# Turning a unit's maxima with VectorE's block transpose in place of a transposing matmul, and writing the rows with eight DMAs

## The chip, the cores and the metric

The kernel runs on one core of a Trainium2 chip. The metric is the device time of one execution in microseconds, the median of several runs. TensorE is called PE here, VectorE DVE, ScalarE ACT, GpSimd POOL, and SyncE, which issues nearly all DMAs, SP.

## The reference

Three things are computed from one input `x` (2048 x 640, float32): multi-head attention with 32 heads of 20 columns, a Fourier mixing (a DFT along the columns and one along the rows, real part), and a sigmoid gate that mixes the two.

```python
qkv = (x @ wqkv).reshape(B, S, 3, H, Dh).transpose(2, 0, 3, 1, 4)
scores = jnp.einsum("bhqd,bhkd->bhqk", q, k) * (Dh ** -0.5)
p = _softmax(scores, axis=-1)
a = (p @ v, heads joined) @ wo
...
y = jnp.einsum("ts,bse->bte", dft_seq_re, a_) - jnp.einsum("ts,bse->bte", dft_seq_im, b_)
return g * a + (1 - g) * y
```

What matters for the change is the softmax: the maximum of each row of scores is needed before the exponentials of that row.

## The kernel before

Attention is cut into 32 **units**, each for two heads (one in partitions 0 to 63, the other in 64 to 127) and half of the 2048 queries. Each unit's scores are computed twice.

The first time (`s_mm`, L158, the kind "m"), queries lie in the partitions: a 60-row matmul gives 128 queries by 512 keys, and DVE reduces it to one maximum per query (L170, into `mx`). A unit takes 32 steps of two such matmuls. When the last is done, `max_nm` (L184) reduces the four partial maxima of each query and negates them: `nm`, 128 partitions by 16 columns, a column for each head h and query tile q.

The second time (`score`, the kind "e", L830), keys lie in the partitions and queries in the columns, so that the exponentials come out as the attention product needs them. The maximum is subtracted inside the matmul: the stacks `qst` (queries) and `kst` (keys) have 62 rows per head there, of which rows 60 and 61 of `kst` are ones and rows 60 and 61 of `qst` hold the negated maximum, split into a rounded part and its remainder, so that no precision is lost in the float32r format. ACT then takes the exponential (L832) and PE multiplies with the values in 16 `av` matmuls (L494).

Between the two stands `max_chain` (L199), which the change touches. It must turn `nm`, which has queries in partitions, into rows of 1024 queries. It takes a PSUM bank, transposes `nm` on PE against an identity (L202), splits the 16 x 128 result in two on DVE (`split`, L108: a copy at L112 and a subtraction at L113, into `m1` and `m2`, which the profile names `m`), and lets SP write each head's eight rows of 128 into row 60 or 61 of `qst` (`rows`, L207 to L211): four DMAs per unit.

The order of the work is written out by hand. A **cycle** is one pass over `ORDER` (L36): eight half-steps of kind "e", eight of kind "m", fifteen fillers "F" (three matmuls or so of the DFT or the output product at a time) and at the end a **burst** "B" (L836). There are 256 cycles; a unit is eight of them. "m" runs 41 steps ahead of "e". In a burst come, in this order: `max_nm` for a unit whose maxima ended, up to two read-outs of finished DFT sums (`run_extras`; on DVE they are L355, L595 or L658), the 16 `av` matmuls, and then `max_chain`. So PE's transpose stands behind the `av` matmuls and ahead of the next cycle's scores. `rows` is issued two steps later, which in SP's own order means as soon as the split is done, because SP runs ahead and waits there. The rows are needed by the "e" step 32n of their unit n, late in the second cycle after the burst.

The scores use five PSUM banks in rotation (`bank`, L122); the transpose takes a place in it. A score of kind "m" gives its bank back when DVE has reduced it, one of kind "e" when ACT has taken its exponentials.

POOL does the preparation for the DFT along the rows: sums and splits of the loaded DFT tiles and of the intermediate tiles (L465, L112 and L113 with POOL, L479, L673), all in SBUF, and the normalisation of the attention output (L524). A hidden DFT fills PE in the first 54 cycles; in these POOL has little to do.

The first unit is turned before the cycles begin; there `max_chain` runs one step after the unit's end and the rows are written at once.

Of the kernel before, what the change touches and what calls it, by code (L numbers as in the profile page):

```python
# [10 lines left out]
F32 = mybir.dt.float32  # L11
R = mybir.dt.float32r
# [6 lines left out]
P = 128  # L19
# [9 lines left out]
KROWS = 3 * DH  # L29
# [38 lines left out]
def f32(ap):  # L68
    return ap.bitcast(F32)
# [3 lines left out]
def mix_kernel(ctx: ExitStack, tc: tile.TileContext, xa, wqk, wb, cdft, wo, out):  # L73
    nc = tc.nc
    pe, act, dve, pool, sp = nc.tensor, nc.scalar, nc.vector, nc.gpsimd, nc.sync
    ctx.enter_context(tc.manual_schedule())

    def pools(**kw):
        return ctx.enter_context(tc.tile_pool(**kw))

    const = pools(name="const", bufs=1)
    small = pools(name="small", bufs=1)
# [14 lines left out]
    ident = const.tile([P, P], F32, name="ident")  # L97
# [10 lines left out]
    def split(dst1, dst2, src, e1, e2):  # L108
        if e1 is act:
            act.activation(dst1, src, AF.Copy)  # L110
        else:
            e1.tensor_copy(dst1, src)  # L112
        e2.tensor_tensor(dst2, src, f32(dst1), op=ALU.subtract)  # L113
# [8 lines left out]
    def bank():  # L122
        return ps_w.tile([P, 512], F32, name=f"ps{next(turn) % 5}")
# [23 lines left out]
    def q_unit(n):  # L147
        u = n % 2 * (S // 2)
        return qst[n // 2 % 2][:, u : u + S // 2]

    mx, nms, ends = {}, {}, []
    now, later = [-1], {}

    def at_step(i, fn):
        later.setdefault(i, []).append(fn)
# [16 lines left out]
    def s_end(i):  # L172
        n, s = divmod(i, 32)
        if n < NU and s == 31:
            if now[0] < 0:
                max_nm(n)
            else:
                ends.append(n)
        if s == 1 and 0 < n <= NU and now[0] < 0:
            max_chain(n - 1)  # L180
# [17 lines left out]

    def max_chain(n):  # L199
        q = q_unit(n)  # L200
        pt = bank()[:16, :P]
        pe.transpose(pt, nms.pop(n), ident)  # L202
        m1 = small.tile([16, P], R, name="m1")
        m2 = small.tile([16, P], R, name="m2")
        split(m1, m2, pt, dve, dve)

        def rows():  # L207
            for h in range(2):
                b = 64 * h + KROWS
                sp.dma_start(f32(q[b : b + 1, :]), f32(m1[8 * h : 8 * h + 8, :]))  # L210
                sp.dma_start(f32(q[b + 1 : b + 2, :]), f32(m2[8 * h : 8 * h + 8, :]))  # L211

        if now[0] < 0:
            rows()
        else:
            at_step(now[0] + 2, rows)
# [619 lines left out]
    def burst(c):  # L836
        for n in ends:
            max_nm(n)
        run_extras(max(done - HIDS, 0) // 3, 2)
        for kt in (2 * c, 2 * c + 1):  # L840
            av_step(now[0], kt // NS, kt % NS)
        while ends:
            max_chain(ends.pop(0))
        if c == HID - 1:
            start_dft()
# [135 lines left out]
```

## Time and profile before

| what | value |
|---|---|
| median of 3 runs | 1891.77 us (1891.42 to 1894.12) |
| span of the profiled execution | 1888.5 us |
| granted TensorE clock | 1.00 |
| first stage, cycles with the hidden DFT | about 255 to 605 us |
| second stage, cycles with the DFT along the rows | about 605 to 1670 us |
| output products beside the last units | about 1670 to 1815 us |

The span is from the first to the last instruction; the measured time has some 3 us around it. In a line of the timeline the first number is the start in us from the span's start, the second the duration in us, then follow engine, line, operation, what it writes and reads with the shapes, how many instructions are merged in it and, in brackets, the idle time of the engine before it and what ended it. "PEld" is PE's loading of weights, which overlaps its matmuls. A line that gives three durations joined by slashes has the shortest, median and longest in ns, and the starts of the first and last instruction in us. A line of the table of stages gives a stretch, its length, the busy time and the number of instructions of PE, PEld, DVE, ACT and POOL, the granted clock, the busy share of the DMA engines and their GB/s. In the lines of the groups the busy time in us and the mean in ns stand behind the first bar, the engine's idle time before them behind the second.

### The profile page before, as it was taken

What the parts mean: (1) busy time and instruction counts of PE and PEld (TensorE: products, weight loads), DVE (VectorE), ACT (ScalarE), POOL (GpSimd) and SP (SyncE); (2) the same over time, 40 slices, a digit from 0 to 9 for tenths busy, and PEclk for the clock granted to TensorE, in tenths of its full rate; (3) what the DMA queues carried; (4) which work ended last, traced back from release to release, by engine and by line L of the source; (5) the groups of instructions that cost most, each with busy time, mean ns of one, the idle gap of its engine ahead of it and who ended that gap; (6) DMA issues with size and microseconds to landing.
All of it is one profiled execution on the core that took longest, in us unless ns stands there. A gap on an engine that the chain in (4) does not pass through costs nothing. (4 is left out here: it accounts for less than half of the span.)

```text
span 1888.5 us, 44537 instructions
## 1 busy us (share of the span) xinstructions
PE 1877.4 (99%) x17453; PEld 1358.2 (72%) x17453; DVE 1470.0 (78%) x2445; ACT 1219.1 (65%) x2350; POOL 1005.1 (53%) x872
## 2 busy tenths in 40 slices
PE   9999999999999999999999999999999999999998
PEld 8987777777776677776767677776767677766666
DVE  4145569989898888888888888888888888889954
ACT  4221147777777767666767667666767676677785
POOL 1200001010004999466699989958879988734343
PEclk9999999999999999999999999999999999999999
DMA  7843341221215575536557576736475746442214
GB/s 232 181 133 128 128 154 48 62 76 49 75 58 147 163 238 178 148 123 169 180 176 238 171 234 190 201 119 189 156 220 195 225 147 205 154 114 70 62 49 157
DMA packets 174804, 280.50 MB, mean 149 GB/s; under 512 B 44303, under 2 KB 106895, under 8 KB 174595
## 3 DMA queue, kind: packets, MB, share of 16 engines
q1 hardware_dynamic: 173635, 275.70, 47.7%
q0 software_dynamic: 960, 1.97, 0.6%
q8 instruction: 137, 2.24, 0.5%
q14 instruction: 72, 0.59, 0.1%
HBM read 213.37 MB, written 63.52 MB: 147 GB/s over the span
## 5 line engine op out<-in xcount | busy, mean ns | idle before, releaser
L170 DVE TENSOR_REDUCE mx<-ps 128x1 f32<-128x512 f32 x2048 | 1294.8, 684 | 175.8 <-PE ps L168 154.8
L832 ACT ACTIVATE p<-ps 128x512 f32<-128x512 f32 x2048 | 1087.0, 599 | 432.7 <-PE ps L168 223.6
L168 PE MATMUL ps<-kst,qst 60*128 60x512 f32 x2048 | 785.2, 415 | 3.7 <-DVE mx L170 1.7
L830 PE MATMUL ps<-qst,kst 62*128 62x512 f32 x2048 | 698.9, 413 | 0.5 <-ACT p L832 0.3
L575 PE MATMUL yp<-a,part 64*128 64x320 f32 x5376 | 649.1, 307 | 0.0
L575 PEld LDWEIGHTS yp<-a,part 64*128 64x128 f32 x5376 | 582.2, 186 | 7.3
L494 PE MATMUL av<-p,v 128*21 128x512 f32 x4096 | 491.3, 596 | 0.0
L830 PEld LDWEIGHTS ps<-qst,kst 62*128 62x128 f32 x2048 | 335.7, 185 | 200.9 <-DVE mx L170 182.4
L168 PEld LDWEIGHTS ps<-kst,qst 60*128 60x128 f32 x2048 | 371.2, 184 | 24.7 <-DVE mx L170 9.6
L113 POOL TENSOR_TENSOR part<-raw,part 128x1024 fp32r<-128x1024 f32 (+1 forms) x129 | 290.4, 2251 | 10.3
L494 PEld LDWEIGHTS av<-p,v 128*21 128x21 f32 x4096 | 98.4, 100 | 226.7 <-issue 223.2
L346 PE MATMUL yp<-wb,xs 64*128 64x320 f32 x1920 | 236.0, 308 | 0.1
L112 POOL CAST part<-raw 128x1024 fp32r<-128x1024 f32 (+1 forms) x129 | 127.0, 985 | 161.5 <-PE yp L575 141.2
L346 PEld LDWEIGHTS yp<-wb,xs 64*128 64x128 f32 x1920 | 206.0, 186 | 4.5 <-DVE raw L355 0.5
L465 POOL TENSOR_TENSOR raw<-raw,raw 128x1024 f32<-128x1024 f32 x77 | 185.4, 2408 | 6.4 <-DMA raw<-in_cdft 4.8
L112 POOL CAST wb<-raw 128x966 fp32r<-128x966 f32 (+1 forms) x4 | 3.4, 862 | 255.4 <-DMA raw<-in_wb 255.4
L524 POOL TENSOR_TENSOR o<-o,rb 128x512 f32<-128x512 f32 x31 | 40.2, 1296 | 146.6 <-DMA rb<-r_scr 100.8
L113 POOL TENSOR_TENSOR a<-araw,a 128x320 fp32r<-128x320 f32 x112 | 97.6, 872 | 9.0
L113 DVE TENSOR_TENSOR p<-ps,p 128x512 fp32r<-128x512 f32 x40 | 27.5, 691 | 93.5 <-ACT p L110 90.8
L646 PE MATMUL yp<-a,part 64*128 64x320 f32 x720 | 89.5, 309 | 0.0
L110 ACT ACTIVATE p<-ps 128x512 fp32r<-128x512 f32 x40 | 23.7, 597 | 100.6 <-PE ps L118 100.6
L646 PEld LDWEIGHTS yp<-a,part 64*128 64x128 f32 x720 | 76.9, 186 | 2.5
(86 smaller groups left out, 1237.0 us busy)
## 6 DMA issues: line engine op xcount, KB each, us to landing
raw<-in_cdft SPq DMA_DIRECT2D x192, 512.0 KB
araw<-a_scr SPq DMA_DIRECT2D x192, 160.0 KB
qk_scr<-p SPq DMA_DIRECT2D x40, 512.0 KB
kst<-qk_scr SPq DMA_DIRECT2D x90, 160.0 KB
qst<-qk_scr SPq DMA_DIRECT2D x90, 160.0 KB
a_scr<-raw SPq DMA_DIRECT2D x64, 160.0 KB
yt<-y_scr SPq DMA_DIRECT2D x64, 160.0 KB
y_scr<-yt SPq DMA_DIRECT2D x64, 160.0 KB
```

What stands on the lines that cost most here:

```text
L112: e1.tensor_copy(dst1, src)
L113: e2.tensor_tensor(dst2, src, f32(dst1), op=ALU.subtract)
L168: pe.matmul(ps, q[b : b + KROWS, qt * P : (qt + 1) * P], k[b : b + KROWS, kc * 512 : (kc + 1) * 512], start=True, stop=True)
L170: return lambda: dve.tensor_reduce(mx[n][:, h, qt, kc : kc + 1], ps, axis=AX.X, op=ALU.max)
L346: pe.matmul(yp[h][:, :HE], xs[r, xz, d, cs], w[r, wz, d, :HE], start=d == 0 and z == 0, stop=d == ND - 1 and z == 2)
L465: pool.tensor_tensor(raws[0], raws[0], raws[1], op=ALU.add if PRODUCTS[n][0][1][0] > 0 else ALU.subtract)
L494: pe.matmul(av[32 * j : 32 * j + DH + 1, :], v[:, kt, h * (DH + 1) : (h + 1) * (DH + 1)], pp[qc][:, h, :], start=kt == 0, stop=kt == NS - 1)
L524: pool.tensor_tensor(o, o, rb, op=ALU.mult)
L575: pe.matmul(yp[h][:, :HE], c[r, cz, cs], a[r, az], start=s == 0 and z == 0, stop=s == NS - 1 and z == 2)
L646: pe.matmul(yp[h][:, :HE], o[r, oz, d], wos[d, hf][r, wz], start=d == 0 and z == 0, stop=d == ND - 2 and z == 2)
L830: pe.matmul(pt, k[b : b + KROWS + 2, kt * P : (kt + 1) * P], q[b : b + KROWS + 2, qc * 512 : (qc + 1) * 512], start=True, stop=True)
L832: act.activation(pts[n, kt, qc][:, h], pt, AF.Exp, scale=float(DH) ** -0.5)
```

## The change

`max_chain` splits first and turns afterwards. The split (copy and subtraction, both on DVE) now works on `nm` as it lies, 128 partitions by 16 columns, and puts the two parts side by side into `mt`, 128 by 32 columns in the order head, part, query tile. One DVE transpose turns each of the four blocks of 32 x 32 within itself into `tr`. PE's transpose and its PSUM bank are gone.

A block holds a quarter of each query tile, so a row of `qst` is put together from four blocks. For each head and each block one DMA writes both parts: 16 partitions of `tr` by 32 columns into rows 60 and 61, as 16 pieces of 32 numbers. That makes eight DMAs per unit in place of four with eight pieces of 128 numbers. What is computed stays the same.

```diff
     def max_chain(n):
         q = q_unit(n)
-        pt = bank()[:16, :P]
-        pe.transpose(pt, nms.pop(n), ident)
-        m1 = small.tile([16, P], R, name="m1")
-        m2 = small.tile([16, P], R, name="m2")
-        split(m1, m2, pt, dve, dve)
+        nm = nms.pop(n)
+        mt = small.tile([P, 2, 2, 8], R, name="mt")
+        split(mt[:, :, 0], mt[:, :, 1], nm.rearrange("p (h q) -> p h q", h=2), dve, dve)
+        tr = small.tile([P, 32], F32, name="tr")
+        dve.transpose(tr, f32(mt).rearrange("p h z q -> p (h z q)"))
 
         def rows():
             for h in range(2):
-                b = 64 * h + KROWS
-                sp.dma_start(f32(q[b : b + 1, :]), f32(m1[8 * h : 8 * h + 8, :]))
-                sp.dma_start(f32(q[b + 1 : b + 2, :]), f32(m2[8 * h : 8 * h + 8, :]))
+                r = 64 * h + KROWS
+                row = f32(q[r : r + 2, :]).rearrange("z (q b p) -> z b q p", q=8, b=4)
+                for b in range(4):
+                    c = 32 * b + 16 * h
+                    sp.dma_start(row[:, b], tr[c : c + 16, :])
```

## The prediction

> **What bounds the kernel now.** I read the page's busy times first, then the stages, then one stretch of the timeline around the edit.
>
> ```profile
> PE 1877.4 (99%) x17453; PEld 1358.2 (72%) x17453; DVE 1470.0 (78%) x2445; ACT 1219.1 (65%) x2350; POOL 1005.1 (53%) x872
> ...
> 255.00:605.00 350.00, 349.08 (x3390) 247.85 (x3388) 309.38 (x520) 253.58 (x498) 35.06 (x26) 1.00 0.27 79
> 605.00:1670.00 1065.00, 1064.98 (x10692) 752.40 (x10686) 894.29 (x1487) 744.32 (x1422) 859.66 (x703) 1.00 0.58 180
> ```
>
> PE is busy nearly throughout, so what is taken out of PE's own order shortens the run, if nothing takes its place. DVE works 88% of the first long stage (309.38 of 350) and 84% of the second. POOL sleeps in the first (35.06 of 350 us) and works 81% of the second (859.66 of 1065). That difference decides this case, I think.
>
> The next rows are two neighbouring cycles. A cycle ends with a burst of 16 `av` matmuls. The burst at 906.64 ends a unit, and the turn of its maxima follows there; the one at 900.32 doesn't.
>
> ```profile
> 900.32 1.92 PE L494 MATMUL av<-p,v 128*21 128x512 f32 x16
> ...
> 902.16 0.18 PEld L830 LDWEIGHTS ps<-qst,kst 62*128 62x128 f32 x1 [0.85 <-DVE mx L170]
> ...
> 902.73 5.13 DVE L170 TENSOR_REDUCE mx<-ps 128x1 f32<-128x512 f32 x8 [1.16 <-PE ps L168]
> ...
> 904.83 0.18 PEld L168 LDWEIGHTS ps<-kst,qst 60*128 60x128 f32 x1
> ...
> 906.64 1.92 PE L494 MATMUL av<-p,v 128*21 128x512 f32 x16
> ...
> 907.71 2.39 POOL L113 TENSOR_TENSOR part<-raw,part 128x1024 fp32r<-128x1024 f32 x1
> 907.77 0.21 DVE L184 TENSOR_REDUCE nm<-mx 128x16 f32<-128x64 f32 x1
> 908.17 0.49 DVE L595 TENSOR_TENSOR m<-yp,m 128x320 f32<-128x320 f32 x1 [0.19 <-ACT m L594]
> 908.49 0.09 PEld L202 LDWEIGHTS ps<-ident,nm 128*16 128x16 f32 x1 [0.85 <-DVE nm L184]
> 908.49 0.28 PE L202 MATMUL ps<-ident,nm 128*16 128x128 f32 x1
> 908.70 0.18 PEld L830 LDWEIGHTS ps<-qst,kst 62*128 62x128 f32 x1
> ...
> 908.80 0.28 DVE L112 CAST m<-ps 16x128 fp32r<-16x128 f32 x1
> ...
> 909.12 0.28 DVE L113 TENSOR_TENSOR m<-ps,m 16x128 fp32r<-16x128 f32 x1
> ...
> 910.05 0.88 POOL L673 TENSOR_TENSOR yt<-yt,m 128x320 f32<-128x320 f32 x1
> ...
> 913.17 1.91 PE L494 MATMUL av<-p,v 128*21 128x512 f32 x16
> L202 PE MATMUL ps<-ident,nm x32: 276/277/278, 226.1 to 1816.4; 128*16 128x128 f32 x32
> ```
>
> From burst to burst the plain cycle takes 906.64 - 900.32 = 6.32 us, the unit's 913.17 - 906.64 = 6.53. The turn thus costs PE 0.21 us: its 0.28, less what overlaps the last `av` matmul. `nm` is ready at 907.98 (907.77 + 0.21), before the burst is over, so PE doesn't really wait for it there.
>
> **What goes from PE.** Thirty-one of the 32 units end in such a cycle (the first is turned before the cycles begin): 31 x 0.21 = 6.5 us gained. The most that it can be is the whole instruction, 32 x 0.277 = 8.9. The turn's PSUM bank also leaves the rotation of five, so the next scores take over banks one place earlier in the order, those of reductions that are over before the burst ends; that costs nothing.
>
> **What DVE does instead.** A copy and a subtraction on 16 x 128 from PSUM (0.28 each) become a copy and a subtraction on 128 x 16 and a transpose of 128 x 32, all in SBUF.
>
> ```profile
> L436 DVE TENSOR_SCALAR gate<-gate x1: 165/165/165, 327.2 to 327.2; 128x16 f32<-128x16 f32 x1
> L113 DVE TENSOR_TENSOR part<-raw,part x12: 692/826/827, 5.1 to 1876.8; 128x640 fp32r<-128x640 f32 x10, 128x512 fp32r<-128x512 f32 x2
> L170 DVE TENSOR_REDUCE mx<-ps 128x1 f32<-128x512 f32 x2048 | 1294.8, 684 | 175.8 <-PE ps L168 154.8
> ```
>
> From 512 to 640 elements the subtraction grows by 134 ns, 1.05 ns an element, so its fixed part is about 155 ns: 0.17 us for 16 elements, which L436 agrees with for the copy (0.165). No row shows a DVE transpose. By the same line 32 elements take 0.19; from above I bound it by the reduction's 0.68; I take 0.19, whose form is nearest. With two gaps of 0.04 (909.12 - 908.80 - 0.28) the three last 0.17 + 0.17 + 0.19 + 0.08 = 0.61 us.
>
> Is that hidden? In the plain cycle the first reduction starts at 902.73, which is 2.41 after its burst began, so without the turn it is due at 909.05. A little lateness is free: the fifth `m` score loads its weights at 904.83 and needs the bank of the third reduction, over at 902.73 + 3 x 0.64 = 904.65, so 0.18 us are free. Where DVE also reads a result out (L595 here, done at 908.66), the three end at 909.3, 0.25 late: 0.07 lost. Where it does not, they end near 908.6 and are hidden by the rest of the burst. Going through the 31 units, 16 have such a read-out: 7 in the first stage (a hidden-DFT sum), 7 with L595, 2 with L658. 16 x 0.07 = 1.1 us. With a transpose of 0.68, 16 x 0.56 = 9.0.
>
> **The wait I forecast.** The new copy and subtraction have all their operands in SBUF, while POOL works there. The trace has one place where DVE does a subtraction-like instruction with both inputs in SBUF beside a busy POOL:
>
> ```profile
> 1870.90 0.68 DVE L938 TENSOR_TENSOR o<-o,rb 128x512 f32<-128x512 f32 x1
> 1869.27 1.75 POOL L884 TENSOR_TENSOR a<-a,m 128x320 f32<-128x320 f32 x2
> 1871.00 1.25 POOL L872 TENSOR_SCALAR p<-p,ngate 128x640 f32<-128x640 f32 x1
> L662 POOL TENSOR_SCALAR a<-a,ngate x30: 522/534/557, 1689.4 to 1857.9; 128x320 f32<-128x320 f32 x30
> L514 DVE RECIPROCAL lc<-lc x31: 241/243/245, 342.3 to 1834.8; 128x16 f32<-128x16 f32 x31
> ```
>
> POOL's 320 columns take 0.53 us, so 640 can't be over 1.07; they took 1.25, 0.18 or more too long, exactly while DVE's 0.68 ran (to 1871.58). [...] In the other direction, DVE behind POOL, the trace shows nothing: L938 itself came late enough, 0.12 before the record of POOL's instruction ended. Against it stands L514, one input from SBUF: 0.24 us each of 31 times, in stages where POOL works most of the time. So the subtraction waits between nothing and the rest of POOL's instruction, and the copy too. For both I take the upper end, less 0.1 us, since L938 was let in 0.12 before a record's end: the subtraction has L938's form, and POOL's own instruction at L872 has just one tensor from SBUF and was held up, so one input alone doesn't keep an instruction clear. This is a choice, and the rivals are its other outcomes.
>
> [...]
>
> Worked through at 907.98: DVE is free at 908.66, POOL subtracts till 910.10. The copy goes then, 910.10 to 910.27. POOL's next instruction (0.88) was waiting and gets in first, till 911.15; then subtraction, gap, transpose: 911.55. Due was 909.05: 2.5 late, 2.3 lost after the free 0.18. A unit without a read-out:
>
> ```profile
> 958.46 0.21 DVE L184 TENSOR_REDUCE nm<-mx 128x16 f32<-128x64 f32 x1
> ...
> 959.98 0.67 DVE L170 TENSOR_REDUCE mx<-ps 128x1 f32<-128x512 f32 x1
> 956.52 2.38 POOL L113 TENSOR_TENSOR part<-raw,part 128x1024 fp32r<-128x1024 f32 x1
> 958.86 0.86 POOL L479 TENSOR_TENSOR araw<-araw 128x320 f32<-128x320 f32 x1
> ```
>
> Copy at 958.90, POOL till 959.93, three done at 960.33; due was 959.98 less the 0.21 and the 0.06 by which today's split delays it, 959.71: 0.62 late, 0.44 lost. Done so for every unit, with the 0.1 off each wait: 7 units with L595, 0.8 to 2.8, mean 1.9, 13.3 us; 2 with L658, 0.9 each, 1.8; 14 without a read-out, 0 to 0.4, mean 0.2, 2.8; the 7 of the first stage only their 0.07, since POOL sleeps; the last has no more reductions behind it. Sum 18.4 us.
>
> Who waits behind: the reductions on DVE, behind them PE for banks, and ACT for PE. POOL's own delay (0.2 us an instruction) is lost in its idle time.
>
> **The rows on SP.** Four DMAs a unit become eight, each of 16 pieces instead of 8.
>
> ```profile
> L210 SPq DMA_DIRECT2D qst<-m x64: 634/658/797, 228.7 to 1818.5; - x64
> L211 SPq DMA_DIRECT2D qst<-m x64: 634/635/653, 229.5 to 1819.1; - x64
> L916 SPq DMA_DIRECT2D raw<-o x4: 706/720/793, 1871.6 to 1874.0; - x4
> 909.11 0.68 SPq L210 DMA_DIRECT2D qst<-m  x1
> 919.13 0.42 PE L830 MATMUL ps<-qst,kst 62*128 62x512 f32 x2
> 1226.25 0.54 SPq L508 DMA_DIRECT2D l_scr<-o  x1
> 1227.98 0.31 SPq L511 DMA_DIRECT2D lc<-l_scr  x1
> ```
>
> From the first issue to the score that needs the rows there are 10.0 us. A small store had landed 1.2 us after its issue ended (L511 waits for L508). I price an issue at 0.66, at most L916's 0.79: 8 x 0.66 + 1.2 = 6.5, at most 7.5. It fits. What follows on SP (`rb`, then the loads for POOL) is 4 x 0.66 = 2.6 us later, which stays off PE while POOL has room (19% of the stage). Cost: nothing.
>
> **Sum.** -6.5 + 18.4 (the 1.1 of above is contained in it) = +11.9 on a span of 1888.5. The three runs' median, 1891.77, lies 3.3 above the span, so I add the change to it: 1904 after rounding.
>
> **Rivals.**
> (1) Only one of the two waits, or DVE gets both instructions in before POOL's next. Then a unit's delay is one rest of a POOL instruction: at 907.98 it is 2.5 - 0.9 = 1.6. Over the units about 9 us: -6.5 + 9 = +2.5, **1894**. For: L514; against: L872.
> (2) No wait at all, faster: -6.5 + 1.1 = -5.4, **1886**; if all 0.28 goes, 1884. For: no DVE row here was ever prolonged. Against: L872.
> (3) The rows come late: an issue over (10.0 - 1.2)/8 = 1.1 us makes the scores at step 32n wait. At 1.3 us it would be 1.6 x 31 = 50 us, **1941** or more. Against: three rows of SBUF-to-SBUF issue between 0.63 and 0.80.
> (4) It doesn't do what it says: the turn leaves PE, but something else, say a slow transpose near 0.68, fills its 0.21: -6.5 + 9.0 = +2.5, again **1894**, without POOL in it.
>
> **How the numbers follow.** Forecast 0.46 at 1904, its own range 1898 to 1911; (1) 0.18; (2) 0.26; (3) 0.03; (4) 0.07. A measurement can tell 0.2%, 3.8 us, from no change. Faster than 1888.0: (2) and a little of (1), 0.28. Within: most of (1) and (4), 0.18. Slower than 1895.6: forecast, (3), and the rest, 0.54. The range goes from the middle of (2) to the upper end of the forecast: 1885 to 1911.
>
> **What would show it.** L202 is gone and PE's burst-to-burst time in unit cycles is the plain 6.32 where POOL sleeps (first stage). In the second stage the DVE copy or subtraction starts late or lasts long, ending with a POOL record, and unit cycles with L595 reach 8 us. [...]

## The result, and the profile after

The changed kernel took 1915.26 us (median of 4; 1902.50, 1914.82, 1915.70, 1915.72) against 1892.94 us of the kernel before (median of 4 runs beside them, 1891.42 to 1894.68). The ratio is 1.0101, its interval 1.0072 to 1.013: slower by about 1%. That is outside the predicted range (1885 to 1911) on the slow side. The execution with the profile is the one of 1902.5 us, with a span of 1900.5; the other three had spans of 1912.9 to 1913.8 and a mean granted clock of 0.995 to 0.997, where the profiled one had 1.000.

Line numbers behind L205 grow by two in the changed kernel. The page's first line, and the new instructions, each with the shortest, median and longest duration in ns:

```profile
PE 1879.2 (99%) x17421; PEld 1357.8 (71%) x17421; DVE 1485.8 (78%) x2477; ACT 1222.3 (64%) x2350; POOL 1005.4 (53%) x872
...
L112 DVE CAST mt<-nm x32: 161/188/1979, 229.0 to 1826.9; 128x16 fp32r<-128x16 f32 x32
L113 DVE TENSOR_TENSOR mt<-nm,mt x32: 174/176/871, 229.2 to 1827.1; 128x16 fp32r<-128x16 f32 x32
L205 DVE STREAM_TRANSPOSE tr<-mt x32: 211/211/214, 229.4 to 1827.5; 128x32 f32<-128x32 f32 x32
L213 SPq DMA_DIRECT2D qst<-tr x256: 599/610/802, 229.6 to 1832.4; - x128
```

In the first stage, where POOL sleeps, the three instructions cost what was forecast (0.167, 0.175 and 0.211 us against 0.17, 0.17 and 0.19). But the copy took up to 1.98 us and the subtraction up to 0.87. The same unit that the prediction worked through, now on the timelines of PE, DVE and POOL:

```profile
910.49 1.92 PE L496 MATMUL av<-p,v 128*21 128x512 f32 x16
...
915.69 0.49 PE L832 MATMUL ps<-qst,kst 62*128 62x512 f32 x1 [1.47 <-DVE mx L170]
...
918.67 0.63 PE L496 MATMUL av<-p,v 128*21 128x512 f32 x4
...
912.44 1.56 DVE L112 CAST mt<-nm 128x16 fp32r<-128x16 f32 x1
914.03 0.78 DVE L113 TENSOR_TENSOR mt<-nm,mt 128x16 fp32r<-128x16 f32 x1
914.85 0.21 DVE L205 STREAM_TRANSPOSE tr<-mt 128x32 f32<-128x32 f32 x1
...
911.58 2.39 POOL L113 TENSOR_TENSOR part<-raw,part 128x1024 fp32r<-128x1024 f32 x1
913.92 0.87 POOL L675 TENSOR_TENSOR yt<-yt,m 128x320 f32<-128x320 f32 x1
```

The copy ends at 914.00, where POOL's subtraction ends (913.97); the second instruction of DVE ends at 914.81, POOL's next at 914.79. DVE waits for POOL's instruction twice, and the wait stands inside the duration, not ahead of it. Of the 64 copies and subtractions of this profile 25 took over 0.3 us, and each of them ends 27 to 37 ns behind the end of an instruction of POOL. The reductions behind it start at 914.99, PE stands still for 1.47 us, and the cycle takes 918.67 - 910.49 = 8.18 us instead of 6.53.

To see where the time went in the profiled executions, I took the length of each cycle (from the first `av` matmul of one burst to that of the next) less the length of the same cycle in the profile of before, and added these by kind. Us, one profiled execution per column:

```text
                                       changed kernel               nm in  copy   before, 8 DMAs   nm in PSUM,
                              first   second  third   fourth        PSUM   ACT    half    all      early loads
unit cycles, first stage (6)  -1.25   -1.25   -1.21   -1.21        -1.21  -1.29  -0.01    0.00     -1.25
unit cycles, later (25)       +7.71   +8.86  +14.22   +8.70        -4.73  +0.39  -0.19   -0.17     -4.64
cycles next to them           +2.24   +2.24   +1.84   +2.39        +2.22  +1.78  +0.17   +2.74     +2.13
two cycles, 313 and 415 us    +2.67   +2.80   +2.62   +2.58        +2.71  +2.15  +1.73   +2.63      0.00
all else                      +0.60   +2.18   +4.75   +4.72        +3.24  +6.53  +3.63   +3.76     +2.02
span against 1888.5          +12.0   +14.8   +22.2   +17.2         +2.2   +9.6   +5.3    +9.0      -1.7
```

(The first, second, third and fourth profiles of the changed kernel are those of 1902.50, 1905.32, 1912.70 and 1907.68 us. The cycle at the change of stages, near 610 us, stands next to a unit cycle; in the third, the fourth and the last column, where it grew by over 1 us, it is counted under "all else".)

### The profile page after: what moved, and what is told of

It reads as the page before. It is cut to its first block, busy times and chain, and to the rows that moved or that the text cites. A ratio compares the mean times of both kernels' runs of the same rounds, so it can differ in the third digit from the quotient of the medians.

```text
span 1900.5 us, 44673 instructions
## 1 busy us (share of the span) xinstructions
PE 1879.2 (99%) x17421; PEld 1357.8 (71%) x17421; DVE 1485.8 (78%) x2477; ACT 1222.3 (64%) x2350; POOL 1005.4 (53%) x872
## 5 line engine op out<-in xcount | busy, mean ns | idle before, releaser
L832 PE MATMUL ps<-qst,kst 62*128 62x512 f32 x2048 | 703.2, 415 | 8.9 <-DVE mx L170 8.5
L832 PEld LDWEIGHTS ps<-qst,kst 62*128 62x128 f32 x2048 | 338.3, 185 | 236.5 <-DVE mx L170 194.0
L168 PEld LDWEIGHTS ps<-kst,qst 60*128 60x128 f32 x2048 | 371.1, 184 | 25.7 <-DVE mx L170 10.1
L113 POOL TENSOR_TENSOR part<-raw,part 128x1024 fp32r<-128x1024 f32 (+1 forms) x129 | 290.4, 2251 | 10.3
```

What stands on the lines that cost most here:

```text
L168: pe.matmul(ps, q[b : b + KROWS, qt * P : (qt + 1) * P], k[b : b + KROWS, kc * 512 : (kc + 1) * 512], start=True, stop=True)
L832: pe.matmul(pt, k[b : b + KROWS + 2, kt * P : (kt + 1) * P], q[b : b + KROWS + 2, qc * 512 : (qc + 1) * 512], start=True, stop=True)
```

## The experiments

**The changed kernel again, three times.** No edit. What was expected of the first:

> The changed kernel as it is, to see its times spread. Port theory (DVE's copy and subtraction wait for POOL's instructions): the waits depend on where POOL stands, so times between 1902 and 1916 come again, and where the time is near 1915 unit cycles of the second stage show longer or more DVE waits (a copy or a subtraction over 1 us in more than the 9 units that have one in the trace of 1902.5) and a granted clock under 1 where PE stands still. Rival (it is the chip of that day, nothing in the kernel): one narrow cluster of times, and the kernel before moves with it.

1908.32 us (median of 4, 1905.32 to 1914.79), while the kernel before stayed at 1892.36 in 25 runs on the same chip (24 of them between 1889.42 and 1894.72, one of 1911.70 with a mean clock of 0.948); ratio 1.0088 (1.0066 to 1.011). The spread belongs to the kernel, not to the day. This median lies inside the predicted range, so how far the kernel is from the forecast depends on which executions one gets. Of the 64 copies and subtractions, 26 took over 0.3 us here, 25 in the first profile. ("Port theory" is in the expectations the name of this wait and of nothing further; what the two engines share, no run shows.) But there is something new: behind a standstill of 1.86 us at 1529.7 the granted clock is one half for 3.4 us. That cycle took 10.02 us where it took 8.17 in the first profile. Two more executions were profiled for that:

> The changed kernel once more, for a profile near 1915. Theory that follows from the trace of 1903.4 (after a standstill of PE of 1.86 us the granted clock fell to one half for 3.4 us, and that cycle grew from 8.2 to 10.0 us): the time is 1900.5 plus longer DVE waits plus some 1.8 us for each such fall, so a run at 1914 has four to six falls, each just behind a standstill over 1.5 us. Rival (the clock falls without regard to PE's standstills): falls at places where PE did not stand still, or a time near 1914 without falls.

> As the run before it, a second look: the same theories with the same numbers.

1912.7 and 1907.7 us. The first of these, around the unit at 1073 us: its DVE and POOL, the standstill of PE, and the table of three stretches (stretch, length, busy us of PE, PEld, DVE, ACT, POOL, then the granted clock, DMA share and GB/s):

```profile
1073.49 1.00 DVE L112 CAST mt<-nm 128x16 fp32r<-128x16 f32 x1
1074.53 2.29 DVE L113 TENSOR_TENSOR mt<-nm,mt 128x16 fp32r<-128x16 f32 x1
...
1072.08 2.38 POOL L113 TENSOR_TENSOR part<-raw,part 128x1024 fp32r<-128x1024 f32 x1
1074.42 2.36 POOL L467 TENSOR_TENSOR raw<-raw,raw 128x1024 f32<-128x1024 f32 x1
...
1077.69 0.79 PE L832 MATMUL ps<-qst,kst 62*128 62x512 f32 x1 [2.43 <-DVE mx L170]
...
1070.00:1075.00 5.00, 5.00 (x53) 3.16 (x50) 4.75 (x9) 3.37 (x7) 4.86 (x4) 1.00 0.31 107
1077.50:1081.00 3.50, 3.31 (x22) 3.31 (x24) 2.58 (x5) 1.70 (x3) 3.42 (x3) 0.51 0.02 2
1081.00:1085.00 4.00, 4.00 (x40) 2.17 (x39) 2.61 (x5) 1.65 (x4) 2.51 (x2) 1.00 0.27 57
```

DVE got its two instructions between two long ones of POOL, waited out both, and PE stood still for 2.43 us. Right after that the clock is 0.51 of full speed in the second stretch and 1.00 again in the third. This cycle took 10.47 us against the plain 6.31: 4.16 more, of which the standstill is 2.43 and the slow clock the remaining 1.73. The execution of 1912.7 has two such falls behind standstills (2.32 and 2.43 us), that of 1907.7 one (2.48). Each has two more, at about 265 and 613 us, where PE did not stand still for over 1.4 us. So my four to six falls, each behind a standstill, came half true. That a slower execution has more units with a copy or subtraction over 1 us, as I expected of the second, came false: the first profile has eight such units (not nine), the second six, the third and fourth seven and six. What grew is the longest subtraction: 2.29 to 2.32 us in the later three, 0.87 in the first.

**The maxima in PSUM.** If the two instructions wait for POOL because their operands lie in SBUF, an input in PSUM should free them. So `nm` is reduced into a bank of the rotation (the first unit's stays in SBUF); split, transpose and eight DMAs remain as in the changed kernel.

```diff
-        nms[n] = small.tile([P, 16], F32, name="nm", bufs=2)
+        nms[n] = small.tile([P, 16], F32, name="nm", bufs=2) if now[0] < 0 else bank()[:, :16]
```

> nm is reduced into a PSUM bank of the rotation instead of SBUF, so that the copy has no SBUF input and the subtraction one; transpose and eight DMAs stay. Port theory: no copy or subtraction on DVE over 0.3 us, every unit cycle of the second stage at 6.3 us, a span of 1888.5 - 6.5 + 3 (the two stalls behind late loads in the first stage) = 1885, a time near 1888, narrow. Rival (the transpose, the order on DVE or the rows make the loss): unit cycles over 7 us remain and the time stays over 1900.

1891.67 us (median of 10, one of which took 3596.45 us, which no run explains; the ratio is that of the other nine), ratio 0.9997 (0.9988 to 1.0007). Its copies and subtractions:

```profile
L112 DVE CAST mt<-ps x31: 161/168/177, 303.8 to 1818.0; 128x16 fp32r<-128x16 f32 x31
L113 DVE TENSOR_TENSOR mt<-ps,mt x31: 173/174/175, 304.0 to 1818.2; 128x16 fp32r<-128x16 f32 x31
```

The longest copy falls from 1.98 us to 0.18, the longest subtraction from 0.87 to 0.18, and the unit cycles are all at 6.2 to 6.4 us: the table's unit rows give -5.9 us together, against +6.5 in the first profile of the changed kernel. The waits for POOL thus cost 12.4 us there, all in the later 25 units. The time itself lies 3.7 above my 1888. The table shows what I had left out: 2.2 us in the cycles next to the unit cycles, and a fall of the clock near 265 us among "all else".

**The copy on ACT, the subtraction on DVE.** To part the two waits:

```diff
-        split(..., nm.rearrange("p (h q) -> p h q", h=2), dve, dve)
+        split(..., nm.rearrange("p (h q) -> p h q", h=2), act, dve)
```

> The copy is done by ACT, the subtraction stays on DVE with both inputs in SBUF. Port theory: ACT's copy takes 0.2 us whatever POOL does; only the subtraction waits, up to the rest of one POOL instruction; loss about half of the 18 us, time 1892 to 1898. Rival (only the copy waits, the subtraction's 0.8 us are something else): no subtraction over 0.3 us, time near 1888.

1894.92 us (median of 10, up to 1909.39), within what was expected; ratio 1.0014 (0.9986 to 1.0042):

```profile
L110 ACT ACTIVATE mt<-nm x32: 207/216/228, 225.8 to 1825.4; 128x16 fp32r<-128x16 f32 x32
L113 DVE TENSOR_TENSOR mt<-nm,mt x32: 162/343/2128, 228.9 to 1825.6; 128x16 fp32r<-128x16 f32 x32
```

ACT's copy never waits; DVE's subtraction alone still does, up to 2.13 us. The unit cycles of the later stages cost +0.4, so the subtraction's wait is worth 5.1 us (against -4.7) and the copy's wait on top of it 7.3. Both exist. This profile also shows a second kind of long wait on DVE:

```profile
1208.74 0.25 DVE L516 RECIPROCAL lc<-lc 128x16 f32<-128x16 f32 x1 [3.01 <-DMA lc<-l_scr]
...
1209.59 0.50 PE L168 MATMUL ps<-kst,qst 60*128 60x512 f32 x1 [2.77 <-DVE mx L170]
```

The reciprocal of another unit's sums waits at the head of DVE's queue for a small load that SP issued late (at 1203.65, 1.6 us after the burst of that cycle began; in the first profile 3.2 us before it), and the reductions wait behind it. It cost 4.6 us there (two cycles, the clock's fall included) and 2.4 in the profile of the half rows below, none in the first profile.

**Eight DMAs in the kernel before.** Two forms, to price the rows by themselves: half of a row each, and all columns in each.

```diff
-                sp.dma_start(f32(q[b : b + 1, :]), f32(m1[8 * h : 8 * h + 8, :]))
-                sp.dma_start(f32(q[b + 1 : b + 2, :]), f32(m2[8 * h : 8 * h + 8, :]))
+                for z, m in enumerate((m1, m2)):
+                    for k in range(2):
# half rows
+                        sp.dma_start(f32(q[b + z : b + z + 1, 512 * k : 512 * k + 512]), f32(m[8 * h + 4 * k : 8 * h + 4 * k + 4, :]))
# all columns
+                        row = f32(q[b + z : b + z + 1, :]).rearrange("z (q p) -> z q p", q=8)
+                        sp.dma_start(row[:, :, 64 * k : 64 * k + 64], f32(m[8 * h : 8 * h + 8, 64 * k : 64 * k + 64]))
```

> The kernel before, its rows written by eight DMAs of half a row each, nothing else. Theory that the longer issue on SP delays the loads of the DFT weights behind the rows: the two stalls of the first stage appear (a cycle near 7.8 us and one near 7.3 us at 313 and 415 us), 2 to 3 us in all, time about 1895.5. Rival (SP's delay costs nothing): 1892.9 within 0.1%.

> The kernel before, its rows written by eight DMAs of which each touches all columns (half of each query tile), so that the first score of a unit waits for four DMAs of its head, as in the changed kernel, where the run with half rows let it wait for two. Theory that PE's extra instruction for waiting delays the unit's first scores: the cycle behind each unit cycle grows by about 0.1 us (2 to 3 us over the 31 units), besides the 1.7 of the two stalls of the first stage: time near 1897. Rival (the 0.1 us comes from the work on DVE): those cycles stay at 6.27 and 6.31, time as with half rows, 1894.

Half rows: 1894.27 us, ratio 1.0011 (1.0002 to 1.0021). All columns: 1897.71 us, ratio 1.0028 (1.0017 to 1.0039). The time of the half rows alone hardly tells the two expectations apart; the cycles do. In both forms the two cycles of the first stage grow (1.7 and 2.6 us). SP in the kernel before (two lines), then SP, ACT and PE in the changed kernel show why:

```profile
303.20 0.67 SPq L210 DMA_DIRECT2D qst<-m  x1
306.08 0.86 SPq L278 DMA_DIRECT2D raw<-in_wb  x2
...
303.29 5.24 SPq L213 DMA_DIRECT2D qst<-tr  x8
308.57 0.90 SPq L280 DMA_DIRECT2D raw<-in_wb  x2
...
316.08 0.44 ACT L356 ACTIVATE raw<-yp 128x320 f32<-128x320 f32 x1 [1.69 <-POOL wb L113]
...
316.57 0.93 PE L348 MATMUL yp<-wb,xs 64*128 64x320 f32 x2 [0.86 <-ACT raw L356]
```

The eight issues take SP 5.24 us where four took 2.8; the next DFT weights are loaded behind them, POOL splits them later, ACT waits for the buffer that the split reads, and PE for ACT. PE's sequencer, meanwhile, shows the other part (waiting instructions ahead of the scores L830 to L832, in the kernel before, half rows, all columns and the changed kernel in this order, then the bursts around the cycle next to unit 2's, for half rows, all columns and the changed kernel):

```profile
L830 PEldq EVENT_SEMAPHORE  x64: 51/51/51, 258.0 to 1823.1; - x64
...
L831 PEldq EVENT_SEMAPHORE  x128: 51/51/51, 258.3 to 1830.5; - x128
...
L832 PEldq EVENT_SEMAPHORE  x128: 51/51/51, 258.9 to 1832.7; - x128
...
L832 PEldq EVENT_SEMAPHORE  x128: 51/51/51, 258.0 to 1834.3; - x128
...
360.19 1.91 PE L495 MATMUL av<-p,v 128*21 128x512 f32 x16
366.46 1.91 PE L495 MATMUL av<-p,v 128*21 128x512 f32 x16
...
360.83 1.92 PE L496 MATMUL av<-p,v 128*21 128x512 f32 x16
367.21 1.92 PE L496 MATMUL av<-p,v 128*21 128x512 f32 x16
...
358.92 1.91 PE L496 MATMUL av<-p,v 128*21 128x512 f32 x16
365.30 1.92 PE L496 MATMUL av<-p,v 128*21 128x512 f32 x16
```

Both forms have twice as many waiting instructions, but with half rows each score needs the DMAs of its own columns alone, and the cycle stays at 6.27. With all columns in each DMA, the first scores of a unit wait for four DMAs per head, and the cycle takes 6.38, as in the changed kernel. That is 0.11 us in each unit of the first stage and mostly 0.03 to 0.07 later, 2.2 us in all in the changed kernel. The runs show that it comes with the four DMAs; that the waiting instructions themselves take the time is argued.

**A standstill without POOL or DMA.** To see whether the clock's fall comes from the standstill alone, the kernel before got small memsets on DVE behind the split of units 7 to 27, on a tile of their own that nothing reads.

```diff
+        if 7 <= n <= 27:
+            pad = small.tile([P, 256], F32, name="pad")
+            for _ in range(7 + 2 * (n % 3)):
+                dve.memset(pad, 0.0)
```

> The kernel before with 7, 9 or 11 small memsets on DVE behind the split of units 7 to 27 (7 units each), so that PE stands still for about 1.5 to 2, 2 to 2.5 and 2.5 to 3 us with no work of POOL in play. Theory that PE's standstill halves its granted clock for a while: no fall behind the shortest, a fall of 3.4 us behind some of the middle and most of the longest, each making that cycle some 1.8 us longer than its standstill does. Rival (the falls in the changed kernel have to do with its waits for POOL or its DMAs): no fall in the whole stage.

1997.99 us. The standstills came out at 2.03, 2.81 and 3.60 us, and the clock fell behind all 21 of them: for 3.4 us after 13 of the 14 shorter, for 6.8 after all of the longest and one of 2.96. One of the shortest:

```profile
1224.70 0.49 PE L834 MATMUL ps<-qst,kst 62*128 62x512 f32 x1 [2.03 <-DVE mx L170]
...
1226.20:1229.60 3.40, 3.40 (x22) 2.30 (x22) 2.84 (x5) 1.44 (x4) 3.26 (x3) 0.50 1.00 367
1230.00:1234.00 4.00, 4.00 (x45) 2.99 (x39) 2.38 (x4) 2.33 (x6) 3.86 (x4) 1.00 0.85 262
```

These unit cycles took 10.1 to 10.3, 11.1 to 11.2 and 12.64 us against 6.52: less the standstill, 1.6 to 2.5 us each for the slow clock (but for the one of 2.96, whose slow clock reaches into the next cycle). The rival falls, and so does my "no fall behind the shortest".

A standstill of 1.86 us (the second profile of the changed kernel, up to 1529.7) is followed by a fall and one of 2.18 us (half rows, from 1205.8 on) is not, and the traces show what parts them. In each trace all falls begin a whole number of 3.413 us apart; in the second profile, those at 264.36 and 1530.70 are 371 such steps apart (1266.34 us / 371 = 3.413). The table of stages, cut along these steps, two for the half rows and two for the second profile:

```profile
1203.97:1207.38 3.41, 1.83 (x22) 1.55 (x18) 1.00 (x4) 2.65 (x6) 3.33 (x3) 1.00 0.83 246
1207.38:1210.79 3.41, 2.81 (x30) 1.87 (x34) 3.41 (x6) 0.94 (x2) 3.27 (x5) 1.00 1.02 255
...
1527.29:1530.70 3.41, 1.55 (x18) 1.14 (x16) 3.38 (x5) 1.42 (x3) 3.27 (x3) 1.00 0.01 3
1530.70:1534.11 3.41, 3.41 (x24) 3.00 (x20) 2.91 (x6) 1.28 (x3) 3.41 (x3) 0.50 0.02 3
```

The 2.18 us lie across a border, 3.41 - 1.83 = 1.58 us of idle PE in one step and 0.60 in the next; the 1.86 us (3.41 - 1.55) lie in one. Counted over the traces of all these runs, 26 steps at full clock have PE idle for 1.80 us or more, 21 of them in the run with memsets, and a fall follows each; of those with up to 1.62 us none is followed by one, except near 265 and 610 us. A slow step was followed by a second one where the standstill reached into it by 0.81 us or more, which is how the 6.8 us come about (0.50 of full speed from 1000.9 to 1007.7 us, where PE works 5.88 of the 6.80 us). No run moved a standstill against the steps on purpose.

**The loads ahead of the rows.** On top of the maxima in PSUM, the two loads of DFT weights are issued four steps earlier, ahead of the rows on SP; their split stays where it was.

```diff
-            if c + HEAD in (NS, 2 * NS):
-                at_step(i + 2, load_wb(3 + (c + HEAD) // NS, pool, pool))
+            if c + 1 + HEAD in (NS, 2 * NS):
+                at_step(i + 6, load_wb(3 + (c + 1 + HEAD) // NS, pool, pool))
```

> nm in PSUM as before, and the two loads of DFT weights of the first stage issued four steps earlier, ahead of the rows on SP. Theory that the rows hold these loads up: the cycles at 313 and 415 us fall from 7.8 and 7.5 back to about 6.3, 2.7 us less: time near 1888, faster than both kernels by 0.2%. Rival (POOL or the raw tiles make the stall): those two cycles stay over 7 us, time 1890.6.

1889.11 us (median of 11, 1887.97 to 1893.07) beside 1893.13 of the kernel before, ratio 0.9984 (0.9975 to 0.9993). The table's row of the two cycles is 0.00. With both edits the block transpose is worth a little: 0.16% faster than the kernel before, and 19 to 26 us below the two medians of the change as it was made (1908.32 and 1915.26, each beside other runs of the kernel before). The earlier loads were not tried in the kernel before, whose two cycles are plain ones (6.26 and 6.28).

## Why the prediction was wrong, point by point

**PE's gain: right.** 6.5 us were forecast. Where POOL can't interfere, unit cycles fell by 5.9 us in all (maxima in PSUM, 31 cycles), to the length of plain ones. Two of the 31, at 1717 and 1766 us, were at the plain length before (6.31 us) and had no 0.21 to give.

**DVE's own work: right in size, its lateness too large.** 0.61 us was forecast for the three, 0.63 came (0.167 + 0.175 + 0.211 and two gaps). The 1.1 us of lateness don't appear: unit cycles of the first stage, which all have a read-out, are plain ones.

**The wait for POOL: right in its form, the term too large.** There is none in the first stage; in six units of the first profile both instructions took over 0.3 us, the next instruction of POOL getting in between. For the unit worked through, 2.3 us of loss were forecast; its cycle is 8.18 against the plain 6.31, 1.9. Over all units 18.4 was forecast, 12.4 measured in the first profile. Against the run with the maxima in PSUM, the seven units with L595 (now L597) lost 8.6 us where 13.3 was forecast (only two of them waited twice); the two with L658, nothing where 1.8 was; the 14 without a read-out, 3.6 where 2.8 was. The row that I took it from shows the other direction, POOL's 1.25 us beside L938; that DVE waits for the rest of POOL's instruction was a choice that no row of before shows. The trace of after shows it: the 1.56 and 0.78 us end with POOL's instructions (914.00 and 913.97, 914.81 and 914.79), as do the other 23 over 0.3 us, and with the input in PSUM both take at most 0.18. By what means the one holds up the other, no run shows.

**"It fits. ... Cost: nothing": the step that failed first.** I priced the issue on SP well (0.66 forecast, 0.61 measured) and asked whether the rows arrive in time, which they do. Of what stands behind them on SP I looked only at POOL's room in the second stage, not at the weights of the first, whose delay reaches PE through a shared buffer: 2.7 us. What the added DMAs ask of the engine that waits for them I didn't price at all: another 2.2 us in PE's order. In the first profile these 4.9 us hid how much smaller the wait was than forecast. Its sum is -5.9 + 12.4 + 4.9 and 0.6 of all else: +12.0 on the span against my +11.9 is luck, an agreement of sums, not of terms.

**The sum itself: the second step that failed.** It added DVE's lateness to the time as if PE ran on at once, and it has no term for the clock. Behind a standstill of 1.8 us or more within one step of 3.41 us the granted clock also fell to one half in these runs (0.50 from 1530.70 on, 0.51 from 1077.50 on): 1.4 to 1.9 us more behind each of the four in the changed kernel's profiles, 1.6 to 2.5 in the run with memsets. Whether a wait reaches that length depends on where POOL stands; the first profile has no such fall, and the executions with falls have spans of 1903.4, 1905.7 and 1910.7. My range was made for unknown waits in one execution, not for this second price. But the clock behind standstills is only a part: of the 10.2 us between the first and the third profile it is 3.6, the rest of the unit cycles, longer waits above all, 2.9, and the other 3.7 lie outside the unit cycles, most of them beside the falls near 265 and 613 us that no long standstill precedes. The three executions with spans near 1913 were not traced, so what put them there, and with them the median outside the range, is argued from the third profile. A fall of 3.4 us at half clock lowers the mean by 0.0009, so their 0.997 stands for three or four falls and 0.995 for five or six, among them those without a standstill and the part of one that ends every trace (from 1898.59 on in the first profile).

**The rivals.** That only one of the two waits exists, (1), is excluded by the copy on ACT; its other form, DVE getting both instructions in before POOL's next, did happen in several units (a copy of 1.85 us and a subtraction of 0.18 at 759.2, 1.98 and 0.18 at 1524.8), which is part of why the wait came out below the forecast. No wait, (2), by the maxima in PSUM; rows too late, (3), and a dear transpose, (4), by 0.61 us an issue and 0.211 us. The 1941 of (3) leaves the 6.5 us of PE's gain out; with it the 50 us give 1935.

## What to carry to other kernels

Before VectorE takes over small work, ask which memory its operands lie in and what GpSimd does at that moment: 16 columns cost 0.17 us from PSUM in all 31 units, and from SBUF anything up to 2.3 us beside a busy GpSimd. A stall of the busiest engine, PE here, had two prices in these runs: its length (2.43 us at 1077.69) and, where 1.8 us or more of it fell into one step of 3.41 us, the slower clock behind it (1.73 us more there). So bound the longest stall and not only their sum. Count added DMAs at three places: their issue, what stands behind them in the queue, and the waiting instructions of the engine that consumes them.

## What the runs showed of the hardware that was not expected

VectorE's wait for GpSimd stands inside its recorded duration (a copy of 0.167 us in the first stage recorded as 1.98 us at 1524.8), not as idle time ahead of it, so a view of waits doesn't list it; the spread between the shortest and longest of a group does (161 to 1979 ns).

The granted clock fell in steps of 3.41 us or twice that, to one half. The standstills of 1.46 to 1.48 us in the first profile were followed by no fall, one of 1.86 by one, one of 2.18 (half rows) by none, and each of the 21 of 2.03 or more in the run with memsets by one: what parts them in these traces is the idle time within one step of a grid of 3.413 us, with the border between 1.62 and 1.80 us. Falls near 265 us, and in some runs near 610 us, came without such a standstill; their cause stays open. They are probably not the changed kernel's own: the kernel before, in its 21 runs beside the last experiments, has mean clocks from 0.998 to 1.000 at times from 1890.40 to 1896.01 us.

A PE waiting instruction is 51 ns long here (L832), but four DMAs instead of two ahead of the first scores of a unit made that cycle 0.11 us longer in the first stage (6.27 to 6.38).
